# A wait and a split load in the stream of keys and values: SyncE issues head 2's keys once most of head 1's values have landed

## The chip, the cores and the metric

The kernel runs on one core of a Trainium2 chip. The metric is the device time of one execution in microseconds (us). The core has five engines with instruction streams of their own: TensorE (PE), VectorE (DVE), ScalarE (ACT), GpSimd (POOL) and SyncE (SP), and 16 DMA engines that carry every transfer. SP computes nothing here. It issues the large loads, one after the other, and waits on semaphores between them.

## The reference, cut to what matters

One token is decoded: layer norm, attention over a long cache, and a small dense block with a Mish activation.

```python
def _A_ref(x, k_cache, v_cache, wq, wo):        # x 1x1x512, H = 32, Dh = 128, caches 1x32x32768x128 bf16
    q = (x @ wq).reshape(B, Sq, H, Dh)...
    scores = jnp.einsum("bhqd,bhkd->bhqk", q, k_cache) * (Dh ** -0.5)
    p = _softmax(scores, axis=-1)
    o = jnp.einsum("bhqk,bhkd->bhqd", p, v_cache)
    return o...reshape(B, Sq, H * Dh) @ wo
...
h = x + _A_ref(_layernorm(x), A_k_cache, A_v_cache, A_wq, A_wo)
h2 = h + _B_ref(_layernorm(h), B_w1, B_b1, B_w2)   # (h@w1+b1) -> Mish -> @w2
```

The caches are 32 heads of 8 MB of keys and 8 MB of values; together with the weights 548 MB are read, each byte once.

## The kernel before, in words

`ring` in SBUF has six slots of 4 MB. `HOMES` gives them fixed owners: the two halves of a head's keys have a slot each (`("k", h, 0)` and `("k", h, 1)`), a head's values have two adjoining slots as one buffer (`("v", h)`), `wq` and later `w1`/`w2` share one, and `wo` has the last. So there is one buffer for each half of the keys and one for the values, and a load for head h+1 can be issued as soon as head h has been read out of the same slot.

The list `order` sets the order of the loads: `wq`, then for each head key half 0, key half 1, values, then `wo`, `w1`, `w2` in pieces. SP walks through it. Before each load it waits for what `freed_by` names (the last transpose of that key half of the head before, or the last value product of the head before); then `start` issues one DMA that adds 16 to the semaphore of the slot, `ready[slot]`, one for each DMA engine. A load of 128 partitions is spread over all 16 DMA engines, each with an equal share. The first four loads wait for nothing.

PE, DVE and ACT run a hardware loop, one round for a head (`S.rounds`). PE transposes the keys in 32 groups of 8 tiles (`k_group`, line 456), DVE copies each group to SBUF (459), PE multiplies it by the query (`scores`, 433); then come the maximum, the exponentials (ACT, 502) and 256 matmuls with the values (`pv`, 470). `pv` waits at tile 0 for `ready_wait(("v", h))` and at tile 128 for `s_half >= 16 * (h + 1)`. Only the last head needs that second wait: its values come in two loads, and the second adds to `s_half`. Since all rounds are the same instructions, the other 31 heads wait as well, and GpSimd gives them their count at the start, with 31 memsets of the scrap row `skip` that add 16 each (line 374).

Of the kernel before, what the change touches and what calls it, by code (L numbers as in the profile page):

```python
# [13 lines left out]
PE, ACT, DVE, POOL, SP = "pe", "act", "dve", "pool", "sp"  # L14
# [140 lines left out]
def bass_sequential_preLN__mha_block_cached__dense_activation_mish__decode_kernel(  # L155
    nc: bass.Bass,
    A_x: bass.AP,
    A_k_cache: bass.AP,
    A_v_cache: bass.AP,
    A_wq: bass.AP,  # L160
    A_wo: bass.AP,
    B_x: bass.AP,
    B_w1: bass.AP,
    B_b1: bass.AP,
    B_w2: bass.AP,
    out: bass.AP,
):
    build_kernel(nc, A_x, A_k_cache, A_v_cache, A_wq, A_wo, B_w1, B_b1, B_w2, out)


def build_kernel(nc, A_x, A_k_cache, A_v_cache, A_wq, A_wo, B_w1, B_b1, B_w2, out):
    D = A_x.shape[-1]
    Dh = 128
    HD = A_wq.shape[1]
    H = HD // Dh
# [10 lines left out]
    SLOT = TPS * Dh  # L186
# [4 lines left out]
    NE = 4  # L191
    NT = 4
    KEEP = 3
    FJ = F // 128
    FLAST = F - FJ * 128
    W1 = KC * F
    assert HALVES == 2 and KC == 4 and H <= 32 and FLAST > 0
    assert KC * HD == SLOT and H * D == SLOT
    assert W1 + (FJ + 1) * D <= SLOT
    WB = Dh // 32  # L200
# [3 lines left out]
    def sb(shape, dt, name):  # L204
        cm = nc.sbuf_tensor(name, shape, dt)
        t = cm.__enter__()
        allocs.append(cm)
        return t.ap()
# [17 lines left out]
    skip = sb([1, H], F32, "skip")  # L226
# [11 lines left out]
    xp = sb([128, KC], BF16, "xp")  # L238
    b1r = sb([FJ + 1, 128], BF16, "b1r")
    xres = sb([128, KC], F32, "xres")  # L240
    lnx = sb([128, 2, 2, KC], F32, "lnx")
    lns = sb([128, 2, 8], F32, "lns")
    xnT = sb([128, 2, KC], BF16, "xnT")
    hsb = sb([128, 6, FJ + 1], F32, "hsb")
    actT = sb([128, FJ + 1], BF16, "actT")
    outr = ering[:, 0, 0, :]
# [12 lines left out]
    L_REG = hlp[:, 208:208 + 2 * KC]  # L259
    hid_ps = S_ps[:, 0:FJ + 1]  # L260
    X_REG = hlp[:, 204:204 + KC]
# [8 lines left out]
    ready = [sem(f"ready{i}") for i in range(NS)]  # L270
# [3 lines left out]
    s_half = sem("s_half")  # L274
# [8 lines left out]
    order = [("wq", 0)]  # L283
# [7 lines left out]
    def slot_of(what):  # L291
        return HOMES[what[0]] + (what[2] if what[0] == "k" else 0)

    def ready_wait(what):
        return (ready[slot_of(what)], 16 * (what[1] + 1 if what[0] in "kv" else 1))

    def free_name(what):
        return "free" + "_".join(map(str, what))

    def freed_by(what):  # L300
        if what[0] in ("w1", "w2"):
            return [f"qm{H}"]
        if what[0] in "kv" and what[1] > 0:
            return [free_name((what[0], what[1] - 1) + what[2:])]
        return []

    def flat_of(what):
        if what[0] == "v":
            return ring[:, HALVES:2 * HALVES, :].rearrange("p s x -> p (s x)")
        return ring[:, slot_of(what), :]  # L310
# [13 lines left out]
    def program(S):  # L324
        t_ = nc.tensor
        a = nc.scalar
        v = nc.vector
        g = nc.gpsimd
        sp = nc.sync


        def start(dst, src, s):
            S.dma(SP, lambda: sp.dma_start(dst, src).then_inc(s, 16))  # L333

        for what in order:
            slot = slot_of(what)
            S.wait(SP, freed_by(what))
            flat = flat_of(what)
            if what[0] == "wq":
                start(flat, A_wq.rearrange("(p k) n -> p (k n)", k=KC), ready[slot])  # L340
            elif what[0] == "wo":
                j0, j1 = WO_J[what[1]:what[1] + 2]
                start(wo_f[:, j0 * D:j1 * D], A_wo.rearrange("(p j) n -> p (j n)", j=32)[:, j0 * D:j1 * D], s_wo[what[1]])
            elif what[0] == "w1":
                k0, k1 = W1_K[what[1]:what[1] + 2]
                start(w1_v[:, k0:k1, :], B_w1[k0 * 128:k1 * 128, :].rearrange("(k p) n -> p k n", p=128), s_w1[what[1]])
            elif what[0] == "w2":
                j0, j1 = W2_J[what[1]:what[1] + 2]
                if j1 <= FJ:
                    start(w2_v[:, j0:j1, :], B_w2[j0 * 128:j1 * 128, :].rearrange("(j p) n -> p j n", p=128), s_w2[what[1]])  # L350
                else:
                    start(w2_v[0:FLAST, FJ, :], B_w2[FJ * 128:F, :], s_w2[what[1]])
            else:
                cache = A_k_cache if what[0] == "k" else A_v_cache
                rows = cache[0, what[1], :, :].rearrange("(p r) d -> p (r d)", r=SCOLS)
                at = what[2] * SLOT if what[0] == "k" else 0
                if what == ("v", H - 1):
                    start(flat[:, 0:SLOT], rows[:, 0:SLOT], ready[slot])
                    start(flat[:, SLOT:], rows[:, SLOT:], s_half)
                else:  # L360
                    start(flat, rows[:, at:at + flat.shape[-1]], ready[slot])
        S.dma(SP, lambda: sp.dma_start(out[0, 0, :].rearrange("(c m) -> c m", c=KC), outr[0:128:32, :]).then_inc(s_out, 16),
# [7 lines left out]
            a.preload_act_table_set("natural_log_exp_and_others")  # L370
        S.step(POOL, lambda: g.iota(identi[:, :], [[-1, 128]], base=0, channel_multiplier=1), name="iota")
        if S.emit and S.only == POOL:
            for n in range(H - 1):
                g.memset(skip[:, n:n + 1], 0.0).then_inc(s_half, 16)
        S.step(POOL, lambda: g.iota(seli[:, :, :], [[-1, WB], [1, 128]], base=0, channel_multiplier=-WB), name="seli")
        S.step(POOL, lambda: g.memset(b1r[:, :], 0.0), name="b1z")
        S.dma(POOL, lambda: g.dma_start(b1r[0:FJ, :], B_b1[0:FJ * 128].rearrange("(j p) -> j p", j=FJ)).then_inc(s_b1, 16),
              waits=["b1z"])
        S.dma(POOL, lambda: g.dma_start(b1r[FJ:FJ + 1, 0:FLAST], B_b1[FJ * 128:F].rearrange("(o p) -> o p", o=1)).then_inc(s_b1, 16))
        S.step(DVE, lambda: v.memset(oT[:, :], 0.0), name="oTz")  # L380
        S.step(DVE, lambda: v.memset(onesm[:, :], 1.0), name="consts0")
        S.step(DVE, lambda: v.memset(epsc[:, :], EPS), name="epsc")
# [54 lines left out]
        def flush(keep):  # L437
            while len(pend) > keep:
                scores(*pend.pop(0))

        def k_group(h, half, gi):
# [20 lines left out]
            pend.append((h, half * TPS + gi * GT, bg))  # L462
            flush(KEEP)

# [78 lines left out]
        for j in range(32):  # L543
            for c in range(KC):
                waits = ["oX"] if j == 0 and c == 0 else []
                if c == 0 and j in WO_J:
# [4 lines left out]
                    start=(j == 0 and c == 0), stop=last, skip_group_check=True),  # L551
# [8 lines left out]
        for kc in range(KC):  # L560
            for j in range(FJ + 1):
# [4 lines left out]
                    start=False, stop=last, skip_group_check=True),  # L566
# [9 lines left out]
        for j in range(FJ + 1):  # L576
# [4 lines left out]
            for c in range(KC):  # L581
# [3 lines left out]
                    start=False, stop=(j == FJ), skip_group_check=True),  # L585
# [5 lines left out]
    log = {}  # L591
    counted = _Sched(nc, False, events, sems, log)
    program(counted)
    with nc.Block() as block:
        for eng_name, attr in ((POOL, "gpsimd"), (SP, "sync"), (DVE, "vector"), (ACT, "scalar"), (PE, "tensor")):
            emitter = _Sched(nc, True, events, sems, log, only=eng_name)

            def _run(eng, emitter=emitter):
                program(emitter)
            getattr(block, attr)(_run)  # L600
            assert emitter.cnt == counted.cnt
# [31 lines left out]
```

## Time and profile before

| what | value |
|---|---|
| time, median of 3 runs | 1277.61 us (1277.6 to 1277.68) |
| profiled execution: span of its instructions | 1275.6 us |
| bytes read, mean rate over the span | 548.08 MB, 430 GB/s |
| PE busy, DVE busy | 1020.0 us (80%), 716.0 us (56%) |
| loads issued by SP: their queue's share of 16 DMA engines | 99.7% |
| mean granted TensorE clock | 0.769 |

The profiled execution is given by its span, from the first to the last instruction; the runs' times are 2.0 us above it. The page's rows in 40 slices give the busy share of each engine in tenths, "DMA" the mean share of the 16 DMA engines, and GB/s what they moved. In the timeline a row is a group of instructions with its start, its duration and, in brackets, the idle time before it. In the window views of the DMA, the window is cut into 40 slices; a packet is counted where it starts, so slices of a short window swing between nothing and more than 100%.

### The profile page before, as it was taken

Reading aid. Unit: us, or ns where it says so; the run is one execution under the profiler, and the core shown is the slowest. Engines: PE = TensorE matmul, PEld = TensorE weight load, DVE = VectorE, ACT = ScalarE, POOL = GpSimd, SP = SyncE. Lnnn points to the kernel's source line nnn. Section 1 sums busy time; section 2 is a strip of 40 time slices with the busy share of each in tenths; the row PEclk is TensorE's granted clock in tenths of the full one; section 3 lists DMA queues with packets and bytes.
Section 4 is the critical chain, followed back from the end, with each engine's and each line's share of the span. In section 5 each row is a group of like instructions: output and inputs, shape, how many; then the busy total and the mean of one; then the engine's idle time right before and its main releaser. Section 6 shows DMA issues by size and latency. Waiting matters only on the chain.

```text
span 1275.6 us, 53362 instructions
## 1 busy us (share of the span) xinstructions
PE 1020.0 (80%) x25129; PEld 996.3 (78%) x25129; DVE 716.0 (56%) x1246; ACT 20.6 (2%) x70; POOL 3.3 (0%) x40
## 2 busy tenths in 40 slices
PE   3788877879777888777887778797778887788977
PEld 3688877879777878777887778797778887777876
DVE  3466544566545665445665446664456654456643
ACT  0000000000000000000000000000000000000000
POOL 1000000000000000000000000000000000000000
PEclk9788777787767887768886778877678877688866
DMA  9999999999999999999999999999999999999998
GB/s 417 416 429 439 434 434 428 432 432 439 432 436 424 436 432 439 432 428 428 438 442 430 427 430 431 437 444 427 430 428 432 440 439 427 424 434 433 438 427 350
DMA packets 16906, 548.24 MB, mean 430 GB/s; under 512 B 1952, under 2 KB 3328, under 8 KB 4096
## 3 DMA queue, kind: packets, MB, share of 16 engines
q1 hardware_dynamic: 16680, 548.09, 99.7%
q8 instruction: 8, 0.13, 0.0%
q10 hardware_dynamic: 152, 0.00, 0.0%
q0 software_dynamic: 64, 0.00, 0.0%
q14 instruction: 2, 0.02, 0.0%
HBM read 548.08 MB, written 0.00 MB: 430 GB/s over the span
## 4 chain that ended last, share of the span: by engine, by line
DMA 66%; PE 32%; SPq 1%; issue 1%; DVE 0%; ACT 0%; ACTq 0%
DMA ring<-in_A_k_cache_dram 65%; PE tps L456 25%; PE sps L433 6%; SPq L333 1%; DMA ring<-in_B_w_dram 1%; PE ops L470 1%; DVE ering L459 0%; PE hlp L492 0%; PE hlp L497 0%; PE tps L583 0%; DVE pmax L482 0%; PE hlp L507 0%; PE yps L485 0%; DVE ering L589 0%; DVE gmax L494 0%
## 5 line engine op out<-in xcount | busy, mean ns | idle before, releaser
L459 DVE COPY ering<-tps 128x1024 bf16<-128x1024 bf16 x1024 | 669.3, 691 | 129.3 <-PE tps L456 128.5
L456 PE MATMUL tps<-identb,ring 128*128 128x128 bf16 x8192 | 667.7, 232 | 76.4 <-DMA ring<-in_A_k_cache_dram 76.4
L456 PEld LDWEIGHTS tps<-identb,ring 128*128 128x128 bf16 x8192 | 522.0, 104 | 78.9 <-DMA ring<-in_A_k_cache_dram 78.9
L433 PE MATMUL sps<-qcur,ering 128*128 128x1 bf16 x8192 | 343.7, 164 | 11.0 <-DVE ering L459 6.7
L470 PEld LDWEIGHTS ops<-pbuf,ring 128*128 128x128 bf16 x8192 | 229.7, 105 | 134.4 <-issue 132.5
L470 PE MATMUL ops<-pbuf,ring 128*128 128x1 bf16 x8192 | 227.6, 165 | 132.4 <-DMA ring<-in_A_v_cache_dram 127.2
L433 PEld LDWEIGHTS sps<-qcur,ering 128*128 128x128 bf16 x8192 | 308.9, 97 | 14.0 <-DVE ering L459 9.4
L509 DVE RECIPROCAL rtotc<-hlp 128x1 f32<-128x1 f32 x32 | 5.4, 168 | 196.6 <-PE hlp L507 196.6
L477 DVE TENSOR_TENSOR oT<-ops,rtotc 128x1 f32 x32 | 5.1, 161 | 165.7 <-PE ops L470 165.7
L502 ACT ACTIVATE pbuf<-sps,nbias 128x256 bf16<-128x256 f32 x32 | 15.1, 473 | 1223.1 <-DVE nbias L499 1223.1
L497 PEld LDWEIGHTS hlp<-gmax,onesmat 1*128 1x128 f32 x64 | 12.0, 233 | 21.6 <-DVE gmax L494 21.6
L497 PE MATMUL hlp<-gmax,onesmat 1*128 1x1 f32 x64 | 14.8, 297 | 11.9 <-DVE gmax L494 11.9
L482 DVE TENSOR_REDUCE pmax<-sps 128x1 f32<-128x256 f32 x32 | 13.6, 424 | 14.3 <-PE sps L433 14.3
L507 PE MATMUL hlp<-esum,onesmat 128*128 128x1 f32 x64 | 18.1, 352 | 0.0
L485 PE MATMUL yps<-xnT,ring 128*128 128x1 bf16 x128 | 16.3, 172 | 0.0
L492 PE MATMUL hlp<-ident,pmax 128*1 128x128 f32 x64 | 12.4, 275 | 4.7 <-DVE pmax L482 3.4
L507 PEld LDWEIGHTS hlp<-esum,onesmat 128*128 128x128 f32 x64 | 16.1, 312 | 0.0
L494 DVE TENSOR_REDUCE gmax<-hlp 1x1 f32<-1x128 f32 x32 | 8.9, 279 | 11.9 <-PE hlp L492 11.9
L499 DVE TENSOR_SCALAR nbias<-hlp 128x1 f32<-128x1 f32 x32 | 5.0, 158 | 17.7 <-PE hlp L497 17.7
L485 PEld LDWEIGHTS yps<-xnT,ring 128*128 x128 | 12.3, 96 | 2.0
L492 PEld LDWEIGHTS hlp<-ident,pmax 128*1 128x1 f32 x64 | 2.7, 80 | 7.4 <-DVE pmax L482 7.4
L386 PE MATMUL hlp<-identb,xr 4*128 4x4 bf16 x1 | 0.2, 159 | 9.3 <-DMA xr<-in_A_x_dram 9.3
(61 smaller groups left out, 41.2 us busy)
## 6 DMA issues: line engine op xcount, KB each, us to landing
ring<-in_A_k_cache_dram SPq DMA_DIRECT2D x64, 4096.0 KB, 26.7
ring<-in_A_v_cache_dram SPq DMA_DIRECT2D x2, 4096.0 KB, 26.2
ring<-in_A_wq_dram SPq DMA_DIRECT2D x1, 4096.0 KB, 12.3
ring<-in_A_wo_dram SPq DMA_DIRECT2D x1, 1792.0 KB, 34.7
ring<-in_B_w_dram SPq DMA_DIRECT2D x2, 688.0 KB, 17.5
ring<-in_A_wo_dram SPq DMA_DIRECT2D x1, 1280.0 KB, 37.4
ring<-in_B_w_dram SPq DMA_DIRECT2D x2, 512.0 KB, 19.6
ring<-in_A_wo_dram SPq DMA_DIRECT2D x1, 768.0 KB, 38.8
```

The source lines that it names most:

```text
L333: S.dma(SP, lambda: sp.dma_start(dst, src).then_inc(s, 16))
L433: S.step(PE, lambda r=r: t_.matmul(S_ps[:, col0 + r:col0 + r + 1], ering[:, bg % NE, r, :], qcur[:, :], start=True, stop=True), name=(name ...
L456: S.step(PE, lambda r=r: t_.matmul(tb[:, r * 128:(r + 1) * 128], kt[:, gi * GT + r, :], identb[:, :], is_transpose=True, start=True, stop= ...
L459: S.step(DVE, lambda: v.tensor_copy(ering[:, bg % NE, :, :].rearrange("p r d -> p (r d)"), tb[:, :]), name=f"ev{bg}", waits=[f"trb{bg}", f ...
L470: S.step(PE, lambda r=r, last=last: t_.matmul(o_ps[:, 0:1], vt[:, r, :], pbuf[:, r:r + 1], start=(r == 0), stop=last), name=([free_name((" ...
L482: S.step(DVE, lambda: v.tensor_reduce(pmax[:, :], S_ps[:, 0:SCOLS], AXX, ALU.max), name=f"pmax{h}", waits=[f"qkh{h}"], kind="pmax")
L485: S.step(PE, lambda kc=kc: t_.matmul(Q_REG, wq_v[:, kc, bass.ds((S.index(h + 1) % H) * Dh, Dh)], xnT[:, 0, kc:kc + 1], start=(kc == 0), st ...
L492: S.step(PE, lambda: t_.matmul(A_REG, pmax[:, :], ident[:, :], start=True, stop=True), name=f"A{h}", waits=[f"pmax{h}", "ident"], kind="A")
L494: S.step(DVE, lambda: v.tensor_reduce(gmax[:, :], A_REG, AXX, ALU.max), name=f"gmax{h}", waits=[f"A{h}"], kind="gmax")
L497: S.step(PE, lambda: t_.matmul(B_REG, onesm[0:1, :], gmax[:, :], start=True, stop=True), name=f"B{h}", waits=[f"gmax{h}", "consts0"], kind ...
L502: S.step(ACT, lambda: a.activation(pbuf[:, :], S_ps[:, 0:SCOLS], ACTF.Exp, bias=nb[:, :], scale=SC, accum_out=esum[:, :]), name=f"exp{h}", ...
L507: S.step(PE, lambda: t_.matmul(C_REG, onesm[:, :], esum[:, :], start=True, stop=True), name=f"C{h}", waits=[f"exp{h}"], kind="C")
```

## The change

Four edits, all about head 1 (`SYNC_H`):

- SP, ahead of the load of head 2's first key half, also waits for `ready` of head 1's values.
- Head 1's values come in two loads: tiles 0 to 231, which add to `ready`, and the last 24 tiles (`TAIL_T`), which add to `s_half`.
- Hence GpSimd's memsets are split: one at the start (head 0), and 29 for heads 2 to 30 behind a wait for `s_half` to reach 32, which the 24 tiles' load does.
- After the first four loads SP's program branches to a block "loads", whose first instruction is aligned to 256 instruction slots.

```diff
+    SYNC_H = 1
+    TAIL_T = 24
...
-        for what in order:
+        for n, what in enumerate(order):
             slot = slot_of(what)
+            if n == 4 and S.emit and S.only == SP:
+                sp.addr_align(256, offset=0, max_nops=0)
+                sp.br("loads")
+                nc.switch_body("loads", valid_engines=[mybir.EngineType.SP])
             S.wait(SP, freed_by(what))
+            if what == ("k", SYNC_H + 1, 0):
+                S.wait(SP, [ready_wait(("v", SYNC_H))])
             flat = flat_of(what)
...
-                if what == ("v", H - 1):
-                    start(flat[:, 0:SLOT], rows[:, 0:SLOT], ready[slot])
-                    start(flat[:, SLOT:], rows[:, SLOT:], s_half)
+                if what in (("v", SYNC_H), ("v", H - 1)):
+                    cut = SLOT if what[1] == H - 1 else 2 * SLOT - TAIL_T * Dh
+                    start(flat[:, 0:cut], rows[:, 0:cut], ready[slot])
+                    start(flat[:, cut:], rows[:, cut:], s_half)
...
         if S.emit and S.only == POOL:
-            for n in range(H - 1):
+            for n in range(SYNC_H):
                 g.memset(skip[:, n:n + 1], 0.0).then_inc(s_half, 16)
...
+        S.wait(POOL, [(s_half, 16 * (SYNC_H + 1))])
+        if S.emit and S.only == POOL:
+            for n in range(SYNC_H + 1, H - 1):
+                g.memset(skip[:, n:n + 1], 0.0).then_inc(s_half, 16)
```

SP's instructions from head 0's values on, before. `s_tr15` and `s_tr31` are the last transposes of a key half, `s_pv` is the last value product; sizes are partitions x elements.

```order
L333 DMA ring<-in_A_v_cache_dram 128x32768
L333 DMA ring<-in_A_k_cache_dram 128x16384 [waits s_tr15]
L333 DMA ring<-in_A_k_cache_dram 128x16384 [waits s_tr31]
L333 DMA ring<-in_A_v_cache_dram 128x32768 [waits s_pv]
L333 DMA ring<-in_A_k_cache_dram 128x16384 [waits s_tr15]
```

And the same place after; `ready2` is the semaphore of the values' buffer.

```order
L335 DMA ring<-in_A_v_cache_dram 128x32768
L340 ISA
L341 UNCONDITIONAL_BRANCH
L335 DMA ring<-in_A_k_cache_dram 128x16384 [waits s_tr15]
L335 DMA ring<-in_A_k_cache_dram 128x16384 [waits s_tr31]
L335 DMA ring<-in_A_v_cache_dram 128x29696 [waits s_pv]
L335 DMA ring<-in_A_v_cache_dram 128x3072
L335 DMA ring<-in_A_k_cache_dram 128x16384 [waits ready2,s_tr15]
```

The alignment and the branch stand behind the fourth load, head 1's values are two DMAs, and the first load of head 2 has a second wait. Behind it the rows are the same in both programs.

GpSimd's instructions after its setup, before:

```order
L371 IOTA identi 128x128
L374 MEMSET skip 1x1 x31
L375 IOTA seli 32x512
L376 MEMSET b1r 11x128
L377 DMA b1r<-in_B_b_dram 10x128 [waits s_pool]
L379 DMA b1r<-in_B_b_dram 1x16x6
L594 UNCONDITIONAL_BRANCH
```

And after:

```order
L380 IOTA identi 128x128
L383 MEMSET skip 1x1
L384 IOTA seli 32x512
L385 MEMSET b1r 11x128
L386 DMA b1r<-in_B_b_dram 10x128 [waits s_pool]
L388 DMA b1r<-in_B_b_dram 1x16x6
L392 MEMSET skip 1x1 [waits s_half]
L392 MEMSET skip 1x1 x28
L607 UNCONDITIONAL_BRANCH
```

29 memsets moved from ahead of GpSimd's two small loads to behind them and behind a wait; nothing else of GpSimd waits for that.

## The prediction

> **What bounds the kernel now.** I read the page first: the slices, the queues, the chain.
>
> ```profile
> span 1275.6 us, 53362 instructions
> ...
> DMA  9999999999999999999999999999999999999998
> ...
> q1 hardware_dynamic: 16680, 548.09, 99.7%
> ...
> DMA 66%; PE 32%; SPq 1%; issue 1%; DVE 0%; ACT 0%; ACTq 0%
> ```
>
> The DMA engines are busy in every slice, with SP's loads alone. The chain gives PE a third, but that is transposing beside other loads; what counts is when data land. So next the chain in order of time. A group of 32 transposes starts when a head's first key half has landed; these are heads 0, 2 and 31:
>
> ```profile
> 22.78 3.60 PE tps L456 x32
> ...
> 101.90 3.60 PE tps L456 x32
> ...
> 1226.48 3.59 PE tps L456 x32
> ```
>
> From head 2 on a head takes (1226.48 - 101.90) / 29 = 38.779 us for 16.777 MB: 432.6 GB/s, 27.0 GB/s for each of the 16 DMA engines, so 1.21 us for a 32 KB row of a key load. Heads 0 and 1 together took 79.12 us, 1.56 us more than two such heads. The DMA queues by window, 31 to 68 us, then 68 to 1262 us, then 1262 to 1274 us, show what else moved:
>
> ```profile
> q8 instruction: 6, 0.10, 1.0%
> q14 instruction: 1, 0.01, 0.1%
> ...
> q14 instruction: 1, 0.01, 0.0%
> ...
> q8 instruction: 2, 0.03, 1.2%
> ```
>
> Six instruction blocks of 16 KB are fetched while PE goes through its loop for the first time; they ride on the same engines as the data. I read the 1.56 us so: a fetch sets back the one engine it falls on by about 1.5 us, the fetches fall on different engines, and a load has landed when its slowest share has. The spared engines run ahead, and the lead stays to the end. The last 4 us of the DMA, 1269 to 1273 us in slices of 0.1 us, show that spread:
>
> ```profile
> DMA  9999999999999987766656664644533221000000
> GB/s 338 348 338 369 348 348 348 348 348 328 348 379 358 307 277 225 205 164 205 195 184 205 215 215 164 225 164 164 184 113 103 92 82 41 0 0 0 0 0 0
> ```
>
> The engines run dry one after the other from 1270.3 to 1272.4 us. The program ends behind the slowest of them, in the timeline and in SP's waits:
>
> ```profile
> 1272.70 0.28 PEld L583 LDWEIGHTS tps<-ring,actT 128*1 128x1 bf16 x12 [0.41 <-DMA ring<-in_B_w_dram]
> ...
> 1273.57 0.64 SPq L362 DMA_DIRECT2D out_dram<-ering  x1
> ...
> SPq L594 <- DMA out_dram<-ering: 1.0, 1, 1.0
> ```
>
> So the bound is the engine that is last, and it has had no idle time since the start. A change helps only if this engine carries less or runs faster, and costs what it makes this engine wait.
>
> **The wait ahead of head 2's keys.** SP's timeline, and PE's wait for head 1's values:
>
> ```profile
> 0.75 0.42 SPq L333 DMA_DIRECT2D ring<-in_A_wq_dram  x1
> 1.23 0.89 SPq L333 DMA_DIRECT2D ring<-in_A_k_cache_dram  x2
> 2.16 0.67 SPq L333 DMA_DIRECT2D ring<-in_A_v_cache_dram  x1
> 35.20 14.66 SPq L333 DMA_DIRECT2D ring<-in_A_k_cache_dram  x2
> ...
> 75.92 10.68 SPq L333 DMA_DIRECT2D ring<-in_A_k_cache_dram  x2
> 99.69 0.33 SPq L333 DMA_DIRECT2D ring<-in_A_v_cache_dram  x1
> ...
> 92.27 1.84 PE L470 MATMUL ops<-pbuf,ring 128*128 128x1 bf16 x64 [3.04 <-DMA ring<-in_A_v_cache_dram]
> ```
>
> Head 2's keys are issued at 75.92 us and land at 101.9: nearly all of that they stand in the queue. Head 1's values land at 92.2. Their last 24 of 256 tiles are 0.786 MB, 1.82 us at 432.6 GB/s, so the shortened load lands at about 90.4, and the wait moves the issue from 75.92 to 90.4. Queued behind SP's wait are head 2's second key half (ready since 86.6) and head 2's values; the half follows at once and the values are not due before 99.69. PE waits for none of it before 101.9.
>
> What the wait costs is a restart. The nearest row is the kernel's first load, into idle engines. Its window, 1.5 to 5.5 us in slices of 0.1 us, in which a packet shows where it starts:
>
> ```profile
> DMA  0000999999890000000007997790000007999797
> ```
>
> Issued at 0.75, the first packets start from 1.9 to 2.7 and the second ones from 3.6 to 4.2. Less one packet of 1.21 us the engines are at full pace 1.6 to 2.2 us after the issue. Then there is the way from the last byte to the semaphore. The output store's window, 1273 to 1275.6 us, has its packets in slices 28 and 29 of 0.065 us:
>
> ```profile
> GB/s 252 0 0 0 0 0 0 0 0 0 0 0 0 0 0 0 0 0 0 0 0 0 0 0 0 0 0 4 12 0 0 0 0 0 0 0 0 0 0 0
> ```
>
> That is 1274.8, and SP's wait of 1.0 us behind its issue ends at 1275.2: 0.4 us. The last engine therefore idles for 0.4 + (1.6 to 2.2) - 1.82 = 0.2 to 0.8 us. The 24 tiles are 6 KB rows; rows of 1 KB run at some 345 GB/s at the end (above), where the same bytes would take 0.46 us longer. That would only fill idle time, up to the 0.2 to 0.8 us. I take 0.5 us for the restart with the split, bounds 0 and 1.2. The engines that lead idle up to 2 us more, which costs nothing by itself: they would only have been done earlier at the end.
>
> The Trainium skill, DMA: Bandwidth & Descriptors, section on the anatomy of one DMA, puts a fixed 2.0 us on a DMA (measured on GpSimd's path), mostly for the confirmation of the last byte; exposed once and covered by the 24 tiles it would be 0.2 us, at the low end of the rows.
>
> **What the lining up does to the end.** Behind the restart all engines start within the 0.6 to 0.8 us of the start window, no longer spread over 2 us; all are as late as the latest. This takes away the room for later fetches. Before, a 16 KB fetch between 1262 and 1274 us fell on an engine with a lead (the ramp to 1272.4 isn't longer than 1.56 us and the start's 0.6 together), so it cost nothing. After, it falls on an engine without one. The set-back is about 1.5 us if it meets the last engine and 0.9 if it meets one 0.6 us ahead, or nothing if it comes too late to matter (one of the two does, behind the last load). I take 1.0 us, bounds 0 and 1.56, and nothing hides it, since PE's last matmuls wait for that very landing.
>
> **The new block, and GpSimd.** SP's branch comes at 2.83 us, its next load at 35.20: 32 us of cover for a block fetch, and behind that the four loads already queued, 21 MB or 48 us. Without cover it would be the fetch's own few us. The half-size fetch (q14) between 68 and 1262 us I take for SP's, since PE's have the other queue and size, and it goes; it fell on a leading engine, as the head's time did not change, so nothing is won. The Trainium skill, Runtime: NRT & Kernel Launch, section on instruction fetch, says that a taken branch out of the fetched window has to fetch its target first, so one early fetch is added; it would cost 0.7 us, half of 1.5, if it met an engine that PE's fetches meet too. I add nothing for it. GpSimd's memsets:
>
> ```profile
> 1.02 1.08 POOL L374 MEMSET skip<- 1x1 f32 x31
> ```
>
> 29 of them take 1.0 us from about 92.3, and PE needs the first at tile 128 of head 2's values, over 35 us later. Head 1's product starts 1.8 us sooner; PE's time is not what binds. Cost nothing.
>
> **Sum.** The span of 1275.6 us gets 0.5 + 1.0 = 1.5 us; the runs shown lie 2.0 us above the span, so 1277.6 + 1.5 = 1279.1 us, +0.12%. About 0.2%, or 2.6 us, is what a measurement of this kernel can tell from no change: this is within it.
>
> **Rivals.** *The restart isn't covered.* If the 24 tiles are through by the time the semaphore is seen, or the restarted engines are slow for some packets, the last engine idles for the whole 0.4 + 2.2 = 2.6 us, and the fetch's 1.5 comes on top: 1281.7 us, slower. It decides from 2.6 us in sum, that is from an idle time of 1.0 us with a full set-back. For it: only one restart is in the trace, 1.6 us is its best engine. Against: the 24 tiles are queued behind the engine's own share and need 1.8 us wherever it stands. 17%.
>
> *Lined-up engines run faster.* If they share something and the lead is worth having back, the end moves towards the mean engine: half of the 2 us, less the 0.5: 1277.1. To be faster by 0.2% a head would need 0.1 us less. Before the fetches the engines were in line, and wq to head 0's keys took PE from
>
> ```profile
> 13.18 0.24 PE L413 MATMUL yps<-xnT,ring 128*128 128x1 bf16 x4 [2.83 <-DMA ring<-in_A_wq_dram]
> ```
>
> to 22.78: 9.60 us for 4.19 MB, against 38.779 / 4 = 9.69 later. Were that real, it would be 0.09 us a load and some 10 us in all; but PE can start behind the landing of wq, which shortens the 9.60, and a few hundredths of a us of that take most of it away. 7%, of which 4% go beyond 0.2%: 1274.5.
>
> *Nothing lines up*: the lagging engines still have tiles when the new keys come, and the lead stays in part: 1277.7. 10%.
>
> **How the numbers follow.** Forecast 66%, uncovered restart 17%, faster 7%, nothing lines up 10%. The forecast's own range is 1277.6 (both terms at their low ends) to 1280.4 (1.2 + 1.56). With the third rival, the near part of the faster one and the lower half of the uncovered restart, 8 in 10 lie in 1276.8 to 1280.9. Slower by over 0.2%: the uncovered restart, 17%. Faster: 4%. Within: 79%.
>
> **What would show it.** The load of head 2's first keys issued near 90.4 instead of 75.92, its landing at 102.2 to 102.7; 38.78 us a head as before; the DMA share at the end falling within about 1 us instead of 2, but for one engine; no q14 fetch in the middle. A head below 38.7 us, or a landing of head 2's keys later than 103.5, would prove me wrong.

## The result, and the profile after

The changed kernel takes 1279.37 us, median of 20 runs (1279.1 to 1280.3); the kernel before takes 1277.58 us in 20 runs (1277.41 to 1277.68). The ratio is 1.0015, with a 95% interval from 1.0009 to 1.0021: 1.8 us slower, or 0.15%, where 1279.1 us was forecast. The sum came out close; its terms did not, as the profile shows. The page of the profile after:

```profile
span 1277.6 us, 53365 instructions
...
q1 hardware_dynamic: 16824, 548.09, 99.7%
```

The span is 2.0 us longer, and the queue of SP's loads has the same share of the 16 DMA engines as before, 99.7%. The timeline of SP, and SP's waits (engine, releaser: total, times, longest):

```profile
64.79 0.80 SPq L335 DMA_DIRECT2D ring<-in_A_v_cache_dram  x2
90.30 0.80 SPq L335 DMA_DIRECT2D ring<-in_A_k_cache_dram  x2
...
SPq L61 <- DMA ring<-in_A_v_cache_dram: 24.6, 1, 24.6
```

The first keys of head 2 are issued at 90.30 us instead of 75.92, and their second half directly behind. The DMA window from 89 to 95 us (slices of 0.15 us; a packet is counted where it starts) shows the restart:

```profile
DMA  3669769247156099995000060099995000999950
```

The end of head 1's values thins out to 91.1; then the engines begin anew within about 0.7 us, and one, by itself, near 92.5, which is 2.2 us after the issue. From there the starts come in clusters: the engines are in line, but for that one. The trace also has the duration of each packet: where a 32 KB packet takes 1.21 us in the running stream, these sixteen first ones take 1.4 to 2.1 us, as the sixteen first ones of the kernel before do at its start. PE's first transposes of heads 2, 3, 4, 5, 6 and 31, with the landing they waited for:

```profile
103.17 3.59 PE L469 MATMUL tps<-identb,ring 128*128 128x128 bf16 x32 [4.97 <-DMA ring<-in_A_k_cache_dram]
142.10 3.44 PE L469 MATMUL tps<-identb,ring 128*128 128x128 bf16 x32 [2.26 <-DMA ring<-in_A_k_cache_dram]
181.09 3.60 PE L469 MATMUL tps<-identb,ring 128*128 128x128 bf16 x32 [2.33 <-DMA ring<-in_A_k_cache_dram]
219.95 3.59 PE L469 MATMUL tps<-identb,ring 128*128 128x128 bf16 x32 [2.28 <-DMA ring<-in_A_k_cache_dram]
258.69 3.59 PE L469 MATMUL tps<-identb,ring 128*128 128x128 bf16 x32 [2.24 <-DMA ring<-in_A_k_cache_dram]
1228.30 3.59 PE L469 MATMUL tps<-identb,ring 128*128 128x128 bf16 x32 [2.23 <-DMA ring<-in_A_k_cache_dram]
```

Head 2 is 1.27 us later than before (101.90). The next four heads take 38.93, 38.99, 38.86 and 38.74 us, 0.4 us more than four heads before; from head 6 on a head takes 38.78 us as before. The DMA share at the end, 1269 to 1276 us in slices of 0.175 us, and the issue of the output:

```profile
DMA  9999999999999999999997632111111003000000
...
1275.62 0.65 SPq L371 DMA_DIRECT2D out_dram<-ering  x1
```

Where the engines ran dry over 2 us before, nearly all of them stop within 0.7 us now, and one or two go on for another microsecond. From head 31's start to the output's issue it took 1273.57 - 1226.48 = 47.09 us before and takes 47.32 now. So the 2.05 us of this execution are 1.27 for the restart, 0.40 in heads 2 to 5, 0.15 in all later heads and 0.23 at the end.

### The profile page after: what moved, and what is told of

Read it like the earlier page. It is cut to its first block, busy times and chain, and to the rows that moved or that the text cites. A ratio compares the mean times of both kernels' runs of the same rounds, so it can differ in the third digit from the quotient of the medians.

```text
span 1277.6 us, 53365 instructions
## 1 busy us (share of the span) xinstructions
PE 1020.6 (80%) x25129; PEld 996.6 (78%) x25129; DVE 716.3 (56%) x1246; ACT 20.5 (2%) x70; POOL 3.4 (0%) x39
## 3 DMA queue, kind: packets, MB, share of 16 engines
q1 hardware_dynamic: 16824, 548.09, 99.7%
## 4 chain that ended last, share of the span: by engine, by line
DMA 76%; PE 22%; issue 1%; DVE 0%; SPq 0%; ACT 0%; ACTq 0%
DMA ring<-in_A_v_cache_dram 71%; PE ops L483 17%; DMA ring<-in_A_wo_dram 3%; PE tps L469 3%; DMA ring<-in_A_k_cache_dram 2%; PE hlp L520 1%; PE sps L446 1%; SPq L335 0%; PE tps L596 0%; PE sps L577 0%; DVE ering L472 0%; PE yps L562 0%; PE hlp L505 0%; PE hlp L510 0%; DVE pmax L495 0%
```

## The experiments

The theory: the last DMA engine sets the time; the wait makes it idle, and takes from the others the lead that hid later set-backs. The rivals were the other edits (the split, GpSimd, the block), a cost of lining up by itself, and fetches that hold up every load.

**Without the wait** (`e1_no_wait`):

```diff
-            if what == ("k", SYNC_H + 1, 0):
-                S.wait(SP, [ready_wait(("v", SYNC_H))])
```

> The changed kernel without SyncE's wait for head 1's values; the split load, the moved memsets and the new instruction block stay. Restart theory (the 1.8 us are the DMA engines' idle time at the wait and what lining them up brings with it): the load of head 2's first keys is issued near 76 us again, the DMA engines never run dry, the time is within 0.3 us of the kernel before, 1277.3 to 1277.9 us. Rival (the split load, GpSimd's wait or the block fetches cost it): the time stays near 1279.4 us.

Measured: 1277.67 us (11 runs), ratio 1.0 (0.9991 to 1.0009). SP's issue of head 2's keys, and PE's start on them:

```profile
75.81 10.68 SPq L335 DMA_DIRECT2D ring<-in_A_k_cache_dram  x2
...
101.98 1.25 PE L467 MATMUL tps<-identb,ring 128*128 128x128 bf16 x10 [4.12 <-DMA ring<-in_A_k_cache_dram]
```

Before, these were 75.92 and 101.90. The wait is the whole cost; split, memsets and block add nothing that shows in the time.

**Without the new block** (`e2_no_block`): the lines with `addr_align`, `br` and `switch_body` are gone.

> The changed kernel without the aligned block and SyncE's branch. Restart theory: 1279 to 1280 us as with the block; SyncE's half-size fetch in the middle comes back, now with no lead to hide in, and costs 0 to 0.7 us. Rival (the early block fetches made the slowest engine slower, since two of them stand in the first 13 us and one share of the first load lands late): 1278.0 to 1278.6 us.

Measured: 1279.58 us, ratio 1.0015 (1.0006 to 1.0024), as with the block; the rival's 1278.0 to 1278.6 falls. In its profile heads 2 to 5 lose nothing (head 2 starts at 103.38 us, head 6 at 258.51), and the restart costs 1.48. SyncE's half-size fetch is back at 945 us, and no head around it takes longer.

**Less and more cover**: `TAIL_T` 1, 40 and 64 instead of 24.

```diff
-    TAIL_T = 24
+    TAIL_T = 1        # 40, 64
```

> The changed kernel with 1 tile instead of 24 in the second load of head 1's values. Restart theory: nothing covers the restart but 0.08 us, so the last engine idles 1.75 us longer: 1280.9 to 1281.4 us, and head 2's keys land 1.7 us later than in the changed kernel. Rival (the cost is not the idle time of the engine that is last but the lining up): no more than 0.5 us over the changed kernel's 1279.4.

> The changed kernel with 40 tiles in the second load (3.03 us of transfer). Restart theory: that covers the 0.4 + 2.2 us of the restart, the last engine does not idle, the engines ahead lose part of their lead: 1277.6 to 1278.3 us. Rival (one engine gets its part of the new load late by 0.8 us whatever the cover, as in the changed kernel's trace): 1278.4 to 1279.2 us.

> The changed kernel with 64 tiles instead of 24 in the second load (4.85 us of transfer). Restart theory: no engine runs dry, nothing is lined up, the leads stay: 1277.5 to 1278.0 us, head 2's keys land as before the change. Rival (the wait or the split costs whatever its cover): near 1279.4 us.

Measured: 1281.21 us with 1 tile (ratio 1.0030, 1.0019 to 1.0041), 1278.77 with 40 (1.0011, 1.0001 to 1.0020), 1277.61 with 64 (1.0, 0.9991 to 1.0009). The DMA windows from 89 to 95 us with 1 tile and with 64:

```profile
DMA  9000111000000001000000000099996500000099
...
DMA  9929997995277979999559599995595999955595
```

With 40 tiles, from 88 to 94 us, and PE's start on head 2:

```profile
DMA  3869889989895649916934319959950599599905
...
102.60 3.60 PE L469 MATMUL tps<-identb,ring 128*128 128x128 bf16 x32 [1.84 <-DMA ring<-in_A_k_cache_dram]
```

With 1 tile no full packet starts between 89.2 and 92.9; one of these (64 KB) takes 2.4 us at 27 GB/s, so every engine stood idle for over a microsecond, and the early ones for about three. With 64 no slice is empty. So cover decides, from +3.6 us down to nothing. (With 1 tile head 2's keys land only 0.9 us later than in the changed kernel, not 1.7; the rest is the end, below.) But 40 tiles missed the theory's 1277.6 to 1278.3 and met the rival: 3.03 us of transfer should have covered a restart of 2.6 us, and the restart still cost 0.70. The rival's reason, one engine that gets its part late, isn't what this trace shows. The load is issued at 89.31, its first packets start from 90.29 to 91.88, and the last of them directly behind the 40 tiles, whose last packets end at about 91.9. But of the seven that start from 91.6 on, three take 1.7 to 1.9 us instead of 1.21. These 0.5 to 0.7 us are about what the run loses: with the wait covered, slow first packets remain.

With 1 tile the end gives the price of a late fetch in engines that are in line, from 1272 to 1277 us in slices of 0.125 us:

```profile
GB/s 352 360 336 352 352 344 352 352 336 352 344 344 369 344 328 352 352 295 246 172 123 74 33 25 25 16 25 25 25 25 16 0 0 0 131 0 0 0 0 0
...
1277.01 0.65 SPq L371 DMA_DIRECT2D out_dram<-ering  x1
```

All but one stop by 1274.9, and that one goes on for about 1 us, at 16 to 25 GB/s (all 16 moved some 350). PE starts on head 31 at 1228.78, so the last stretch takes 48.23 us, 1.14 more than before. I put it down to the block fetch of 16 KB at 1269.0 us, the only one between 1262 and 1272: its own packet takes 1.08 us, and one engine alone is late. The fetch was not taken away to prove it.

**Four such waits** (`e6_four_syncs`), behind heads 1, 9, 17 and 25, each with its split load, and with GpSimd's memsets divided accordingly:

```diff
+    SYNC_AT = (1, 9, 17, 25)
...
+            if what[0] == "k" and what[2] == 0 and what[1] - 1 in SYNC_AT:
+                S.wait(SP, [ready_wait(("v", what[1] - 1))])
```

> The changed kernel with the wait and the split load at heads 1, 9, 17 and 25 instead of head 1 alone. Restart theory: each further wait costs the last engine its idle time again, and there is no lead left that it could come out of: 0.5 to 1.7 us each, 1281 to 1284.5 us, with no head faster than 38.77 us. Rival (the cost comes once, with the loss of the leads; later waits are covered by the 24 tiles): 1279.1 to 1280 us. Rival (lined-up engines run faster and the leads grow back slowly): below 1279.1.

Measured: 1284.24 us, ratio 1.0053 (1.0039 to 1.0067). Each further wait costs again; nothing grows back, no head is faster. In its profile head 2 starts 1.52 us late, heads 6 to 31 take 2.45 us more for the three other waits, 0.8 each, and the end 1.32. About 1 us more stands behind the issue of the output store (1278.85 us, of a span of 1281.9): SP's next instruction starts 1.05 us after its wait for that store, in the changed kernel 0.06. It is no part of the waits' cost, and why it is there is not known.

**More fetches, with the leads and without** (`e7_before_blocks` on the kernel before, `e8_after_blocks` on the changed one): SP branches to an aligned block at four more places.

```diff
+    FETCH_AT = (30, 42, 54, 66)
...
+            if n in FETCH_AT and S.emit and S.only == SP:
+                sp.addr_align(256, offset=0, max_nops=0)
+                sp.br(f"more{n}")
+                nc.switch_body(f"more{n}", valid_engines=[mybir.EngineType.SP])
```

> The kernel before with four branches of SyncE to aligned blocks, at loads 30, 42, 54 and 66 (heads 9 to 21), so up to eight more fetches of 8 KB. Theory of the leads (a fetch sets one engine back, and one with a lead hides it): 0 to 0.7 us over the kernel before, 1277.5 to 1278.3, most heads at 38.78 us. Rival (a fetch holds up all loads): each costs its 0.3 to 0.7 us, 2 to 5 us in all, 1279.6 or more.

> The changed kernel with the same four branches as in the run beside it (heads 9 to 21). Theory of the leads: the engines are in line, the first fetches set some of them behind the rest, so it costs the changed kernel 0.4 to 1.4 us, 1279.8 to 1280.8, more than the same blocks cost the kernel before. Rival (the leads hide nothing): the same cost as in the kernel before, within 0.2 us.

Measured: 1281.29 us on the kernel before, ratio 1.0029 (1.0017 to 1.0040), outside the 1277.5 to 1278.3 expected and inside the rival's 2 to 5 us; 1283.65 us on the changed one, ratio to the kernel before 1.0045 (1.0032 to 1.0059), where 1279.8 to 1280.8 was expected. The chain of the first, at the heads around the four branches (behind the starts at 334.52, 489.66, 645.76 and 802.31), and its queues from 360 to 842 us:

```profile
334.52 3.59 PE tps L461 x32
373.29 3.60 PE tps L461 x32
...
489.66 3.59 PE tps L461 x32
529.41 3.59 PE tps L461 x32
...
645.76 3.60 PE tps L461 x32
685.97 3.23 PE tps L461 x32
...
802.31 3.59 PE tps L461 x32
842.53 3.44 PE tps L461 x32
...
q14 instruction: 8, 0.07, 0.0%
```

Each branch fetches two blocks of 8 KB. The first pair costs the head nothing (38.77 us), the second 0.97 (39.75), the third and fourth 1.44 each (40.21, 40.22). The DMA from 1270 to 1278 us, in slices of 0.2 us:

```profile
DMA  5677999668710000000000000000000000000020
GB/s 207 217 193 263 340 345 335 222 227 290 227 34 14 15 26 20 26 26 20 26 26 26 20 26 26 20 26 26 20 26 26 15 0 0 0 0 0 0 82 0
```

For 4 us one engine is alone, at the rate of one. So SP's fetches do not spread, as I had assumed: all fell on one engine, 0.72 us each. Its lead hid the first pair and a third of the second: 1.44 + 0.47 = 1.9 us, about the spread seen at the end of the kernel before. So the time met the rival's range, but not its reason: a fetch that holds up all loads would have cost with the first pair too, and would not have left 15 engines done 4 us early. What was wrong was that the fetches spread; that a lead hides a fetch is what the first pair shows. On the changed kernel the same branches cost 4.3 us instead of 3.7. The difference has the expected sign but is small, and the changed kernel's own times spread over 1.2 us. By its heads (0.25 us for the first pair, about 1.4 for each later one) I read that this engine still had 1.2 us on the last one, which is late at the restart.

**The changed kernel twice more**, one profiled execution each (`a1_again`, `a2_again`):

> The changed kernel once more, one look. Theory: what it costs is the restart (head 2's keys at 102.2 to 103.4 us) and, in some runs, a few heads over 38.8 us right behind the lining up, which differ from run to run; hence the wider spread of its times (1279.1 to 1280.3 us against 1277.4 to 1277.7 before). Rival: heads 3 to 5 are slow in every run by the same 0.4 us, as in the first profile.

> The changed kernel a third time, one look; as for the run beside it.

Measured: 1279.86 and 1279.37 us. Head 2 starts at 102.58 and 102.98, inside the range, and the excess of heads 2 to 5 differs (0.40, 0.66, 0.20), so the rival of a fixed 0.4 us falls; but all three profiles have some of it. The terms, from the same rows of the timelines (us more than before; each row is one profiled execution):

| kernel | restart | heads 2 to 5 | heads 6 to 31 | end | sum |
|---|---|---|---|---|---|
| changed | 1.27 | 0.40 | 0.15 | 0.23 | 2.05 |
| again, first | 0.68 | 0.66 | 0.19 | 1.02 | 2.55 |
| again, second | 1.08 | 0.20 | 0.01 | 0.76 | 2.06 |
| without the block | 1.48 | 0.03 | 0.19 | 0.32 | 2.02 |
| 1 tile | 2.20 | 0.00 | 0.10 | 1.14 | 3.44 |
| 40 tiles | 0.70 | 0.03 | 0.16 | 0.18 | 1.06 |
| 64 tiles | 0.12 | 0.02 | 0.09 | 0.09 | 0.32 |
| without the wait | 0.08 | 0.04 | 0.06 | 0.17 | 0.36 |

In the four profiles with one wait and 24 tiles, restart and end move against each other: 1.48 and 1.27 go with 0.32 and 0.23, 1.08 and 0.68 with 0.76 and 1.02. I read it so: where one engine is late at the restart, the fetch at the end hides behind it; where the engines are better in line, the end pays. No run tests this by itself.

## Why the prediction was right

- **The bound** held: the bytes are the same, and the time goes with the DMA engine that is last, as far as the DMA rows tell (they don't name the engines). A head takes 38.78 us with the engines apart or in line. The rival of faster lined-up engines falls: the fastest head behind a lining up takes 38.74 us. *Nothing lines up* is what 64 tiles do: 1277.61 us.
- **The wait**: issue at 90.30 (forecast 90.4), head 2's keys at 103.17, 102.58 and 102.98 by PE's start (forecast 102.2 to 102.7). The restart's term was 0.5 us and measured 0.7 to 1.5. The way to work it out held: the time to the semaphore, plus the time to full pace, less the cover. Two of its steps were too small. The engine that is last decides, so not the middle of the 0.2 to 0.8 us was due but the end. And full pace came not 1.6 to 2.2 us after the issue but up to 2.7 in the first profile, for one engine: its first packet starts at 92.5 and takes 1.67 us, its second starts at 94.19; less 1.21 us and less 90.30 that is 2.68, and 0.4 + 2.68 - 1.82 = 1.26 us, where 1.27 was measured. Why one engine begins late there stays open. With 40 tiles none does, and the slow first packets alone cost 0.5 to 0.7 us; the rival named them ("slow for some packets"). The Trainium skill, DMA: Bandwidth & Descriptors, anatomy of one DMA, with its fixed 2.0 us (for GpSimd's path) would have made this term 0.2 us, an estimate: the runs' 0.7 to 1.5 decide against that here.
- **The end**: forecast 1.0 us, bounds 0 and 1.56; measured 0.2, 1.0 and 0.8, and 1.1 with 1 tile. The full set-back of 1.5 us was over-sized: the most that the end paid is 1.0 to 1.1 us behind one wait, and 1.3 behind four. And the engines were not all as late as the latest, so that the late one could hide part of it. In the first profile this term was over-sized by as much as the restart was under-sized, 0.77 us each. That the sum came out is in part luck.
- **What the sum lacked**: 0.2 to 0.7 us in the first heads behind the lining up. All three profiles of the changed kernel have it, and the one with four more branches (0.46). The run with four waits has the same 24 tiles and the same block and doesn't have it, nor do those without the block, with 1 or with 40 tiles. The cause stays open.
- **The new block and GpSimd** cost nothing that shows (the runs without wait and without block). GpSimd's cover was as named: its 29 memsets stand at 92.18 us and take 1.01 us. The half-size fetch between 68 and 1262 us is gone, as forecast. The block does leave a mark that is made up for: PE starts on head 0 at 23.73 us instead of 22.78 (22.79 without the block), yet without the wait head 2 is back at 101.98. "Different engines" was right for PE's fetches as far as the 1.56 us tell, and wrong for SP's. The Trainium skill, Runtime: NRT & Kernel Launch, on instruction fetch, says that a taken branch has to fetch its target. The trace agrees, with two q14 fetches of 8 KB for each branch: two before 31 us, where the kernel before has none, and eight for the four branches that were added.
- **The uncovered restart** was the right rival for too little cover: 1281.7 forecast for it, 1281.21 measured with 1 tile.

No tried version beats the kernel before; those within its noise are the ones in which no engine ran dry.

## What to carry to other kernels

Where DMA engines are busy from start to end, as here (99.7%), a load lands with its slowest share, and the end belongs to the engine that is last. Evening them out won nothing here, and each point where the queue runs empty cost a restart: 0.7 to 1.5 us with 1.8 us of transfer as cover, 0.7 with 3.0, and 0.1 with 4.85, where no engine ran dry. When you size such a cover, ask for the engine that is last, not for the mean. A lead of some engines looks like waste at the end of a profile, but it hid later set-backs, such as the first pair of added instruction fetches. A sum that comes out is no proof of its terms: read each from its own rows, and in more than one execution.

## What the runs showed of the hardware

An 8 KB instruction fetch of SyncE set one DMA engine back by 0.72 us under full load, and all eight fetches of four branches fell on the same engine, so that the set-backs added up (3.85 us of 5.8 showed in the heads). Behind the wait, with 24 tiles as cover, the last engine's first packet started 1.7 to 2.2 us after the issue in the three profiles of the changed kernel. The first 32 KB packets took up to 2.1 us there instead of 1.21, much as at the start of the kernel before (1.4 to 2.0).
